# A second Strassen level in the up product of a fused attention and expert kernel

## The chip, the cores and the metric

The kernel runs on one core of a Trainium2 chip. The metric is the device time of one execution in microseconds (us); lower is better. Three runs of the kernel before the change gave 1882.01, 1885.54 and 1887.38 us, with a median of 1885.54 us.

## What is computed

The first half is a linear attention: per batch and head a 64x64 matrix `kv`, the queries times it, and a division by the root mean square. The second half sends the 4608 rows of 512 values through four experts, each an up product, a relu and a down product, and adds the four results with weights per row.

```python
kv = np.einsum('bhsd,bhse->bhde', k, v)          # batch 8, heads 8, s 576, d 64
out = np.einsum('bhsd,bhde->bhse', q, kv)
rms = np.sqrt(np.mean(out * out, axis=-1, keepdims=True) + 1e-06)
x = (out / rms * g_norm)                          # then laid out as (4608, 512)
p = domain_probs / (domain_probs.sum(-1, keepdims=True) + 1e-09)
for e in range(4):
    h = np.maximum(x @ w1[e], 0.0)                # 512 -> 1024
    y += p[:, e:e + 1] * (h @ w2[e])              # 1024 -> 512
```

All data is float32, and TensorE is given float32 operands.

## The kernel before

**Chunks and pairs.** The 4608 rows are cut into 9 chunks of 512 (eight batches' first 512 rows, and one chunk of the 64 rows that each batch has left). The work on one expert and one chunk is called a pair here; there are 4 x 9 = 36, numbered `s = 9*e + c`. A pair has an up product (`up`, 512 to 1024) and a down product (`down`, 1024 to 512).

**One Strassen level in both.** Each product is cut in 2x2x2 blocks, and seven block products take the place of eight (the Winograd form, with few additions). For this the operands are needed in sums: `weights_1` and `weights_2` form four sums of 1024 columns for each of the two weights of an expert, `x_forms` four sums of 512 columns for each chunk's x. The x operands of a chunk, seven tiles of 512 columns, are made once, during the first expert, stored to DRAM (`x_kept`) and loaded again by `x_again` for the other three.

**Up.** `up` runs over the seven products `m` in the order 1, 2, 6, 5, 7, 4, 3 and over two halves `i` of the hidden units. One such product is four matmuls with 256 moving columns (L624). Two PSUM banks of a half take the seven products: some products add on top of what stands in the bank. ScalarE copies a bank to SBUF after the products 1, 6 and 7 (L655), VectorE adds such a copy to the other bank (`total`, L647), and ScalarE applies the relu (L640). Four sums of 512 columns then form the down product's operands, on VectorE or GpSimd.

**Down.** `down` runs seven products for each of two halves of the rows, each four matmuls with 256 columns (L749). VectorE scales every result and adds it to the accumulator (`merge`, L704, and L700 where it is the first).

**Order.** Nothing is scheduled by a compiler here. Every operation is put into a `Plan` with a key (its due place), a cost for each engine that may do it, and its buffers. `Plan.layout` goes through time with these costs, starts on each free engine the first ready operation by key, within a reach, and hands out buffers from fixed sets (`SLOTS`: `big` tiles of 1024 columns, `small` of 512, PSUM banks `ub`, `db`, `ab`). The program is written in that order, and each engine then works through its own list strictly in turn. The key of a down product of pair s is s + 1, so it runs between the up products of pair s + 1. An operation with the costs of `either` goes to VectorE or to GpSimd, whichever is free first; all these sums have the line L276.

Of the kernel before, what the change touches and what calls it, by code (L numbers as in the profile page):

```python
# [24 lines left out]
class Op:  # L25
    def __init__(self, key, cost, fn, reads, writes, kb):
        self.key, self.cost, self.fn, self.kb = key, cost, fn, kb
        self.bufs = list(dict.fromkeys(list(reads) + list(writes)))
        self.new = []
        self.deps = {}  # L30
        self.start = self.end = self.eng = None


class Plan:
# [10 lines left out]

    def __init__(self):
        self.ops = []

    def add(self, key, cost, fn, reads=(), writes=(), parts=(), kb=0):
# [6 lines left out]
        for b in writes:  # L56
            if not b.writers:
                op.new.append(b)
# [4 lines left out]
        for b in parts:  # L63
            if not b.writers:
                op.new.append(b)
            b.writers.append(op)
# [4 lines left out]
    def layout(self, slots):  # L71
# [15 lines left out]
        def ready(op, eng):  # L87
# [4 lines left out]
            for b in op.bufs:  # L92
                if b.kind is not None and b.ap is None and b not in op.new:
                    return None
# [3 lines left out]
            for b in op.new:  # L98
                if b.kind is not None:
                    need[b.kind] = need.get(b.kind, 0) + 1  # L100
            for k, n in need.items():
                if len(free[k]) < n:
                    return None
# [3 lines left out]
        while left:  # L107
            moved = False
            for eng in todo:
# [8 lines left out]
                for op in pending:  # L118
# [11 lines left out]
                    if eng == "SP":  # L130
                        busy[eng] = t + op.cost[eng]
                        bus = max(bus, t + 1.5) + op.kb / 170.0
# [3 lines left out]
                    for b in op.new:  # L136
                        if b.kind is not None:
# [28 lines left out]
def kernel(  # L166
# [63 lines left out]
    SLOTS = {"big": 20, "small": 46, "kv": 6, "kvbd": 8, "ss": 4, "rt": 4, **BANKS}  # L230
    SHAPE = {"big": 2 * NT, "small": NT, "kv": 2 * KR * D, "kvbd": P, "ss": H, "rt": H}
# [10 lines left out]
        (c, m): dram.tile([P, NT], F32, tag=f"x{c}_{m}", name=f"x{c}_{m}")  # L242
# [9 lines left out]
    def pe(columns, passes=2):  # L252
        return {"PE": passes * columns * 2.02 / 2400 + 0.003}
# [63 lines left out]

    def w1_src(e, dh, uh):
# [7 lines left out]
    def weights_1(e, key, step):  # L326
# [19 lines left out]
        w1f[e] = f  # L346
# [69 lines left out]
    def attention(b, key, span, rem):  # L416
# [3 lines left out]
        for hp in range(NPAIR):  # L420
# [29 lines left out]
            plan.add(at(hp), pe(4 * P, 1), turn, reads=[qt], writes=[bank])  # L450
# [22 lines left out]
            plan.add(at(hp), pe(12 * D), key_values, reads=[kt, vt], writes=[bank])  # L473
# [9 lines left out]
            plan.add(at(hp + 0.4), pe(NT), attend, reads=[qT, kvbd[hp]], writes=[raw])  # L483
# [9 lines left out]
            plan.add(at(hp + 1), pe(4 * P, 1), turn_x, reads=[x], writes=[bank])  # L493
# [26 lines left out]
        plan.add(at(NPAIR - 1), pe(4 * P, 1), turn_rem, reads=[qr], writes=[tb])  # L520
# [7 lines left out]
        def attend_rem(eng):  # L528
# [7 lines left out]
            at(NPAIR), pe(NT), attend_rem, reads=[qTr] + [kvbd[hp] for hp in range(NPAIR)],  # L536
# [13 lines left out]
        plan.add(at(NPAIR + 1), pe(4 * P, 1), turn_xrem, reads=[xr], writes=[xb])  # L550
# [15 lines left out]
    def two(ap):  # L566
        return ap.rearrange("p (k t) -> p k t", k=2)

    def x_forms(c, key, step):
        xh = x_halves(c)  # L570
        f = {m: Buf("small", f"xf{c}_{m}") for m in (5, 6, 7, 4)}
        lo, hi = slice(0, HN), slice(HN, NT)
        views = {
            1: (xh[0], lambda: two(xh[0].ap[:])[:, :, lo]),
            12: (xh[0], lambda: two(xh[0].ap[:])[:, :, hi]),
            2: (xh[1], lambda: two(xh[1].ap[:])[:, :, lo]),
            3: (xh[1], lambda: two(xh[1].ap[:])[:, :, hi]),
        }
        for m in (5, 6, 7, 4):
            views[m] = (f[m], lambda m=m: two(f[m].ap[:]))  # L580
        for j, (o, a, b) in enumerate(((5, 12, 1), (6, 3, 5), (7, 3, 12), (4, 2, 6))):
            combine(
                key + j * step, either(NT), views[o][1], views[a][1], views[b][1], ALU.subtract,
                [views[a][0], views[b][0]], [views[o][0]],
            )
        for m in range(1, 8):
            kept[c, m] = Buf(None, f"kept{c}_{m}")
            plan.add(
                key + 0.5, SPC,
                lambda eng, m=m: nc.sync.dma_start(out=two(x_kept[c, m][:]), in_=views[m][1]()),  # L590
# [240 lines left out]
```

## Time and profile before

| what | value |
|---|---|
| runs | 1882.01, 1885.54, 1887.38 us |
| the profiled execution | 1884.76 us, its span 1883.0 us |
| TensorE weight loads (PEld) busy | 1629.1 us of the span, 9472 of them |
| VectorE (DVE) busy | 624.3 us |
| ScalarE (ACT) busy | 390.9 us |
| GpSimd (POOL) busy | 376.4 us |
| moved by DMA | 178.81 MB |

A row of the page's groups reads: line, engine, operation, tile written and tiles read, shape, count, then busy time in total and mean nanoseconds of one, and after the bar the idle time of the engine just before it with what ended that. A float32 matmul is two TensorE instructions in the trace, called passes here, each with its own weight load; so the 2016 matmuls of `up` are 4032 passes. A matmul's end in the trace is modelled, and consecutive ones overlap; the distance from start to start tells how fast they follow each other.

### The profile page before, as it was taken

The page shows a single profiled execution, that of the slowest core. Times are in us where ns is not written, and L with a number is a line of the kernel's source. Part 1 is how long each engine was busy: PE and PEld are TensorE (multiplying, and loading weights), DVE is VectorE, ACT ScalarE, POOL GpSimd, SP SyncE. Part 2 cuts the span into 40 slices and gives each one's busy share as a digit, 9 for nine tenths or more (in the row PEclk, how much of TensorE's full clock was granted, in tenths as well). Part 3 has the DMA queues.
Part 4 walks back from the last instruction along what each step waited for, and adds up shares of the span by engine and source line. Part 5 has one row for each costly group of instructions (what it writes and reads, how often), then busy time and mean ns, then how long its engine had stood idle before and what let it go on. Part 6 is the DMA issues. An engine that isn't in the chain of part 4 may idle for free.

```text
span 1883.0 us, 23222 instructions
## 1 busy us (share of the span) xinstructions
PE 1858.1 (99%) x9472; PEld 1629.1 (87%) x9472; DVE 624.3 (33%) x978; ACT 390.9 (21%) x697; POOL 376.4 (20%) x277
## 2 busy tenths in 40 slices
PE   6999999999999999999999999999999999999999
PEld 5888888888888888888888888888888888888887
DVE  3433333333333333333333223323333333323323
ACT  2433322332111111111111111111111111111110
POOL 2523232224222111111222100001222111111111
PEclk7999999999999999999999999999999999999999
DMA  9544233314232222222322222222332222222111
GB/s 235 154 138 129 78 114 109 105 42 151 73 118 84 84 84 84 84 84 94 109 102 94 77 80 84 80 83 95 118 129 84 84 84 84 84 84 84 45 34 34
DMA packets 142074, 178.81 MB, mean 95 GB/s; under 512 B 49424, under 2 KB 76816, under 8 KB 141968
## 3 DMA queue, kind: packets, MB, share of 16 engines
q1 hardware_dynamic: 141968, 177.33, 29.6%
q8 instruction: 75, 1.23, 0.3%
q14 instruction: 31, 0.25, 0.0%
HBM read 123.02 MB, written 54.26 MB: 94 GB/s over the span
## 4 chain that ended last, share of the span: by engine, by line
PE 97%; SPq 2%; DMA 1%; issue 0%; DVE 0%
PE ub L624 46%; PE db L749 29%; PE ab L749 17%; SPq L282 1%; PE ab L481 1%; PE ab L463 1%; PE ab L491 1%; PE ab L448 1%; PE ab L530 0%; DMA big<-in_moe_w_dram 0%; DMA small<-in_q_dram 0%; SPq L298 0%; PE ab L545 0%; PE ab L515 0%; DVE small L409 0%
## 5 line engine op out<-in xcount | busy, mean ns | idle before, releaser
L624 PE MATMUL ub<-small,big 128*128 128x256 f32 x3600 | 852.4, 380 | 0.0
L624 PEld LDWEIGHTS ub<-small,big 128*128 128x128 f32 x3600 | 681.5, 190 | 93.3 <-issue 0.9
L749 PE MATMUL db<-big,small 128*128 128x256 f32 x2520 | 596.0, 380 | 0.0
L749 PEld LDWEIGHTS db<-big,small 128*128 128x128 f32 x2520 | 475.3, 190 | 64.2 <-issue 0.6
L276 POOL TENSOR_TENSOR small<-small,small 128x512 f32<-128x512 f32 x145 | 210.0, 1456 | 1071.9 <-ACT small L640 1066.3
L749 PE MATMUL ab<-big,small 128*128 128x256 f32 x1512 | 356.2, 379 | 0.0
L749 PEld LDWEIGHTS ab<-big,small 128*128 128x128 f32 x1512 | 287.3, 190 | 39.1
L655 ACT ACTIVATE small<-ub 128x512 f32<-128x512 f32 x216 | 128.8, 597 | 681.4 <-PE ub L624 671.7
L704 DVE SCALAR_TENSOR_TENSOR small<-db,p_all,small 128x256 f32<-128x256 f32 x243 | 117.4, 483 | 453.7 <-PE db L749 453.6
L276 DVE TENSOR_TENSOR small<-ub,small 128x512 f32<-128x512 f32 x216 | 149.4, 692 | 270.3 <-PE ub L624 139.3
L640 ACT ACTIVATE small<-small 128x512 f32<-128x512 f32 x216 | 136.0, 630 | 463.0 <-DVE small L276 463.0
L704 DVE SCALAR_TENSOR_TENSOR small<-ab,p_all,small 128x256 f32<-128x256 f32 x189 | 91.4, 484 | 310.3 <-PE ab L749 310.3
L276 DVE TENSOR_TENSOR small<-small,small 128x512 f32<-128x512 f32 x143 | 160.6, 1123 | 4.6 <-ACT small L640 2.5
L276 POOL TENSOR_TENSOR big<-big,big 128x1024 f32<-128x1024 f32 x26 | 61.1, 2352 | 189.8 <-PE ub L624 105.0
L624 PE MATMUL ub<-big,big 128*128 128x256 f32 x384 | 91.7, 383 | 0.0
L624 PEld LDWEIGHTS ub<-big,big 128*128 128x128 f32 x384 | 71.7, 192 | 9.4 <-issue 0.2
L640 ACT ACTIVATE small<-ub 128x512 f32<-128x512 f32 x72 | 43.0, 597 | 152.1 <-PE ub L624 152.1
L402 POOL TENSOR_TENSOR rt<-ss,mhalf 128x8 f32<-128x8 f32 (+1 forms) x40 | 65.5, 1637 | 3.3
L700 DVE TENSOR_SCALAR small<-db,p_all 128x256 f32<-128x256 f32 x72 | 34.8, 483 | 90.8 <-PE db L749 90.8
L393 DVE TENSOR_REDUCE ss<-small 128x8 f32<-128x512 f32 (+1 forms) x40 | 27.4, 684 | 94.1 <-ACT small L388 94.1
L398 POOL TENSOR_SCALAR ss<-ss 128x8 f32<-128x8 f32 (+1 forms) x40 | 9.4, 236 | 199.3 <-DVE ss L393 198.7
L388 ACT ACTIVATE small<-ab 128x512 f32<-128x512 f32 (+1 forms) x40 | 23.8, 596 | 68.3 <-PE ab L481 54.5
(45 smaller groups left out, 405.7 us busy)
## 6 DMA issues: line engine op xcount, KB each, us to landing
small<-x SPq DMA_DIRECT2D x189, 256.0 KB, 4.3
o<-small SPq DMA_DIRECT2D x108, 256.0 KB, 2.0
small<-o SPq DMA_DIRECT2D x108, 256.0 KB, 3.7
big<-in_moe_w_dram SPq DMA_DIRECT2D x32, 512.0 KB, 5.2
small<-in_q_dram SPq DMA_DIRECT2D x72, 128.0 KB, 3.3
kv<-in_k_dram SPq DMA_DIRECT2D x32, 288.0 KB, 3.4
kv<-in_v_dram SPq DMA_DIRECT2D x32, 288.0 KB, 4.1
x<-small SPq DMA_DIRECT2D x36, 256.0 KB, 2.6
```

The source lines that it names most:

```text
L276: lambda eng: adder(eng).tensor_tensor(out=out_(), in0=a(), in1=b(), op=op),
L282: key, SPC, lambda eng: nc.sync.dma_start(out=dst(), in_=src), reads=reads,
L388: lambda eng: nc.scalar.activation(out=sq.ap[0:n, :], in_=raw.ap[0:n, :], func=ACT.Square),
L393: lambda eng: nc.vector.reduce_sum(out=ss.ap[0:n, :], in_=rows(sq), axis=AX.X),
L402: nc.gpsimd.tensor_tensor(out=rt.ap[0:n, :], in0=ss.ap[0:n, :], in1=mhalf[0:n, :], op=ALU.pow)
L448: nc.tensor.transpose(bank.ap[:, rs], qt.ap[:, rs], ident[:])
L624: nc.tensor.matmul(ps.ap[:, u * HN:(u + 1) * HN], lhsT=two(w1f[e][m].ap[:])[:, kt, cols], rhs=views[m][1]()[:, kt, :], start=(m in (1, 2, ...
L640: lambda eng: nc.scalar.activation(out=b.ap[:], in_=src.ap[:], func=ACT.Relu),
L655: lambda eng, to=banks[i, -m], ps=ps: nc.scalar.activation(out=to.ap[:], in_=ps.ap[:], func=ACT.Copy),
L700: nc.vector.tensor_scalar_mul(out=acc[i].ap[:, cols], in0=ps.ap[:, 0:HN], scalar1=prob)
L704: nc.vector.scalar_tensor_tensor(out=acc[i].ap[:, cols], in0=ps.ap[:, 0:HN], scalar=prob, in1=acc[i].ap[:, cols], op0=ALU.mult, op1=ALU.add,)
L749: nc.tensor.matmul(ps.ap[:, 0:HN], lhsT=src[:, kt % 2, t * P:(t + 1) * P], rhs=w2f[e][m].ap[:, kt * HN:(kt + 1) * HN], start=(m in (1, 2, ...
```

## The change

The up product gets a second Strassen level inside the first. Each of the seven block products of a pair is itself cut in 2x2x2 blocks, now over all 512 hidden units of the block, and computed with seven products of two matmuls with 128 moving columns. A pair has 49 of them.

- **Operands.** `weights_1` forms, for each of the seven outer operands, four more sums of 256 columns: two in place of raw quarters, three results in a new tile `w1y` of 768 columns. `x_forms` forms four more sums of 128 columns for each of the seven x operands (tile `xt`), 28 a chunk. `x_kept` has seven blocks of 128 columns instead of four; `x_again` loads two tiles for each operand, of 384 and 512 columns.
- **Evacuation.** For each outer product ScalarE makes four copies of 256 columns out of PSUM (L710) and VectorE three additions of 256 columns (L718) into one `big` tile.
- **Outer sums.** What the first level did inside PSUM is now done in SBUF: 11 sums of 1024 columns a pair on VectorE or GpSimd (`add` in `up`), which include the forms for the down product, and four relus of 1024 columns (L680).
- **Buffers and the layout.** `big` 28 instead of 20, `small` 22 instead of 46, new sets `w1y` (7) and `snap` (5). The layout may not take the last four `big` or `small` tiles for an operation that lies ahead of TensorE's place, and a buffer gets its slot at its first started writer. The bus of loads is reckoned at 215 instead of 170 kB per us. `down` only reads `h` through another view, and a merge now decides at its place in the order whether it is the first.

The core of the diff:

```diff
@@ Plan
+    SPARE = {"big": 4, "small": 4}
...
             for k, n in need.items():
-                if len(free[k]) < n:
+                if len(free[k]) < n + (self.SPARE.get(k, 0) if op.key > front + 0.1 else 0):
                     return None
...
-                        bus = max(bus, t + 1.5) + op.kb / 170.0
+                        bus = max(bus, t + 1.5) + op.kb / 215.0
@@ buffers
-    SLOTS = {"big": 20, "small": 46, "kv": 6, "kvbd": 8, "ss": 4, "rt": 4, **BANKS}
+    SLOTS = {
+        "big": 28, "w1y": 7, "kv": 4, "small": 22, "snap": 5, "kvbd": 8, "ss": 4, "rt": 4, **BANKS
+    }
...
-        (c, m): dram.tile([P, NT], F32, tag=f"x{c}_{m}", name=f"x{c}_{m}")
+        (c, m): dram.tile([P, 7 * P], F32, tag=f"x{c}_{m}", name=f"x{c}_{m}")
@@ weights_1
+        for j, m in enumerate(OUTER):
...
+            k2 = key + (8 + j) * step
+            for o, a, b, op in (
+                (5, 7, 4, ALU.add), (7, 1, 7, ALU.subtract), (6, 5, 1, ALU.subtract),
+                (3, 2, 6, ALU.subtract),
+            ):
+                combine(
+                    k2, either(HN), parts[o][1], parts[a][1], parts[b][1], op,
+                    [parts[a][0], parts[b][0]], [parts[o][0]],
+                )
@@ x_forms
+        for j, m in enumerate(OUTER):
...
+            for o, a, b in ((5, 12, 1), (6, 3, 5), (7, 3, 12), (4, 2, 6)):
+                combine(
+                    key + (4 + j) * step, either(P), parts[o][1], parts[a][1], parts[b][1],
+                    ALU.subtract, [parts[a][0], parts[b][0]], [parts[o][0]],
+                )
@@ up
-        for j, m in enumerate(ORDER):
-            for i in range(2):
...
-                    for u in range(2):
-                        cols = slice((2 * i + u) * P, (2 * i + u + 1) * P)
-                        for kt in range(2):
-                            nc.tensor.matmul(
-                                ps.ap[:, u * HN:(u + 1) * HN],
-                                lhsT=two(w1f[e][m].ap[:])[:, kt, cols], rhs=views[m][1]()[:, kt, :],
+        for i, m in enumerate(OUTER):
+            whole = made[m] = Buf("big", f"m{n}")
+            bank = {1: Buf("ub", f"u1_{n}"), 2: Buf("ub", f"u2_{n}")}
+            for j, mm in enumerate(ORDER):
+                key = s + (i + j / 7) / 7
+                if mm == 5:
+                    bank[2] = Buf("ub", f"u3_{n}")
+                ps = bank[1 if mm in (1, 6, 7, 4) else 2]
...
+                    for u in range(2):
+                        nc.tensor.matmul(
+                            ps.ap[:, u * P:(u + 1) * P],
+                            lhsT=w1f[e][m][mm][1]()[:, u * P:(u + 1) * P], rhs=views[m][mm][1](),
...
+                if mm in (1, 6, 7):
+                    snap[mm] = Buf("snap", f"s{mm}_{n}")
+                    copy(snap[mm], lambda b=snap[mm]: b.ap[:])
+                if mm == 2:
+                    total(0, 0, ps, snap[1])
+                elif mm == 7:
+                    total(1, 1, bank[2], snap[7])
+                elif mm == 4:
+                    copy(whole, lambda whole=whole: block(whole, 1, 0))
+                elif mm == 3:
+                    total(0, 1, ps, snap[6])
+            key = s + (i + 1) / 7
...
+            if m == 2:
+                add(key, unit(1), made[1], made[2])
+                relu(key, h[1])
+            elif m == 6:
+                add(key, made[1], made[1], made[6])
+            elif m == 5:
+                add(key, made[6], made[1], made[5])
+            elif m == 3:
+                add(key, unit(21), made[6], made[3])
+                relu(key, h[21])
+                add(key, unit(7), h[1], h[21], ALU.subtract)
+            elif m == 7:
+                add(key, made[1], made[1], made[7])
+                add(key, unit(4), made[1], made[5])
+                relu(key, h[4])
+                add(key, unit(5), h[21], h[4])
+                add(key, unit(6), h[5], h[1], ALU.subtract)
+            elif m == 4:
+                add(key, unit(2), made[1], made[4])
+                relu(key, h[2])
+                add(key, unit(3), h[2], h[6], ALU.subtract)
```

### Where the instructions stand

In the rows below a name with a number is one buffer: `ub`, `db` and `ab` are PSUM banks, `small` and the first name after it on an up row are x and weight operands, `x4` or `x2` at the end counts matmuls.

TensorE before, in a pair of the second expert; an up row (L624) alternates with a product of `down` (L749, here in two rows of two):

```order
L624 MATMUL ub3_163<-small36_128,big19_91 128x256 x4
L749 MATMUL ab0_166<-big8_80,small29_121 128x256 x2
L749 MATMUL ab0_166<-big8_80,small22_114 128x256 x2
L624 MATMUL ub0_160<-small27_119,big18_90 128x256 x4
L749 MATMUL ab1_167<-big12_84,small44_136 128x256 x2
L749 MATMUL ab1_167<-big12_84,small2_94 128x256 x2
L624 MATMUL ub1_161<-small27_119,big18_90 128x256 x4
```

TensorE after, in a pair of the second expert (L697 is `up`, L831 `down`):

```order
L831 MATMUL ab1_161<-big18_90,big2_74 128x256 x4
L697 MATMUL ub1_155<-small16_127,big1_73 128x128 x2
L697 MATMUL ub0_154<-small5_116,big13_85 128x128 x2
L697 MATMUL ub2_156<-small5_116,big13_85 128x128 x2
L831 MATMUL ab0_160<-big11_83,big19_91 128x256 x4
L697 MATMUL ub1_155<-small16_127,big1_73 128x128 x2
L697 MATMUL ub3_157<-small4_115,w1y5_105 128x128 x2
L697 MATMUL ub0_154<-small8_119,w1y2_102 128x128 x2
L697 MATMUL ub2_156<-small8_119,w1y2_102 128x128 x2
L831 MATMUL ab1_161<-big5_77,big20_92 128x256 x4
L697 MATMUL ub0_154<-small8_119,big13_85 128x128 x2
```

Two outer products are under way at a time, with two banks each. Between two uses of a bank by consecutive products (`ub0` in rows 3, 8 and 11, `ub2` in rows 4 and 9) there now stand two or three up rows and one down row.

VectorE after, in the first pair of the third expert: evacuations (L718), merges (L788) and outer sums (L276) in one list. `big8` in the sixth row is `h21`, whose relu on ScalarE lies between that row and the eighth.

```order
L788 SCALAR_TENSOR_TENSOR small21_132<-ab1_161,p_all_69,small21_132 128x256
L718 TENSOR_TENSOR big0_72<-ub1_155,snap2_135 128x256
L718 TENSOR_TENSOR big20_92<-ub0_154,snap0_133 128x256
L788 SCALAR_TENSOR_TENSOR small5_116<-ab0_160,p_all_69,small5_116 128x256
L718 TENSOR_TENSOR big0_72<-ub1_155,snap3_136 128x256
L276 TENSOR_TENSOR big8_80<-big9_81,big0_72 128x1024
L788 SCALAR_TENSOR_TENSOR small5_116<-ab1_161,p_all_69,small5_116 128x256
L276 TENSOR_TENSOR big21_93<-big19_91,big8_80 128x1024
L718 TENSOR_TENSOR big20_92<-ub0_154,snap4_137 128x256
L718 TENSOR_TENSOR big0_72<-ub1_155,snap2_135 128x256
L788 SCALAR_TENSOR_TENSOR small5_116<-ab1_161,p_all_69,small5_116 128x256
```

Before, no sum of 1024 columns stood among these; now each is a longer row in front of the evacuations behind it.

VectorE before at the start, between the second and the last scaling of x (L409) of the first chunk:

```order
L409 TENSOR_TENSOR small18_110<-ab0_166,rt1_157 128x512
L393 TENSOR_REDUCE ss2_154<-small20_112 128x8
L409 TENSOR_TENSOR small22_114<-ab1_167,rt2_158 128x512
L276 TENSOR_TENSOR big11_83<-big2_74,big3_75 128x1024
L276 TENSOR_TENSOR big12_84<-big11_83,big0_72 128x1024
L276 TENSOR_TENSOR big13_85<-big1_73,big12_84 128x1024
L393 TENSOR_REDUCE ss3_155<-small24_116 128x8
L409 TENSOR_TENSOR small26_118<-ab0_166,rt3_159 128x512
```

The same place after the change, its first twelve rows of thirty (L432 is the scaling, `ss2` the third head pair's reduction):

```order
L432 TENSOR_TENSOR small17_128<-ab0_160,rt1_151 128x512
L276 TENSOR_TENSOR w1y1_101<-big1_73 128x256
L276 TENSOR_TENSOR big9_81<-big0_72,big2_74 128x1024
L276 TENSOR_TENSOR w1y2_102<-big9_81 128x256
L276 TENSOR_TENSOR big9_81<-big9_81 128x256
L276 TENSOR_TENSOR w1y2_102<-w1y2_102,big9_81 128x256
L276 TENSOR_TENSOR w1y3_103<-big3_75 128x256
L276 TENSOR_TENSOR w1y2_102<-big9_81,w1y2_102 128x256
L276 TENSOR_TENSOR w1y4_104<-big10_82 128x256
L276 TENSOR_TENSOR big3_75<-big3_75 128x256
L276 TENSOR_TENSOR w1y3_103<-w1y3_103,big3_75 128x256
L276 TENSOR_TENSOR w1y3_103<-big3_75,w1y3_103 128x256
```

Between the two scalings there are now 2 sums of 1024 columns and 23 of 256 on VectorE, where there were 3 of 1024 columns.

218 lines of the change are left out of this document (117 added, 101 removed).

## The prediction, made before the changed kernel was run

> **What bounds the kernel now.** I read the page's busy times and slices first, then the chain, then stretches of the span, then TensorE's waits.
>
> ```profile
> span 1883.0 us, 23222 instructions
> PE 1858.1 (99%) x9472; PEld 1629.1 (87%) x9472; DVE 624.3 (33%) x978; ACT 390.9 (21%) x697; POOL 376.4 (20%) x277
> PEclk7999999999999999999999999999999999999999
> PE 97%; SPq 2%; DMA 1%; issue 0%; DVE 0%
> ...
> 20.00:30.00 10.00, 6.01 (x56) 5.35 (x57) 3.14 (x3) 2.85 (x7) 4.14 (x3) 0.67 1.16 262
> 30.00:40.00 10.00, 5.32 (x36) 4.75 (x35) 5.09 (x6) 2.20 (x6) 3.43 (x4) 0.50 0.81 202
> 60.00:100.00 40.00, 38.71 (x316) 33.62 (x315) 18.61 (x27) 16.88 (x36) 21.87 (x21) 1.00 0.59 150
> 520.00:1000.00 480.00, 480.00 (x2226) 422.55 (x2225) 152.92 (x239) 84.95 (x140) 82.23 (x50) 1.00 0.28 95
> ...
> PE ab L491 <- DVE small L409: 10.4, 4, 4.1
> ```
>
> In the stretch rows the columns are PE, weight loads, DVE, ACT, POOL, clock, DMA. TensorE is the bound: 99% busy, 97% of the chain, granted its full clock after the start. Busy is no proof of full speed, but the stretch from 520 to 1000 us is: 2226 passes in 480 us, **215.6 ns a pass**, all of 256 columns, with no gap. TensorE idles only in the first 60 us and a little to 100; its largest wait is 10.4 us there, for x. So time comes off only by fewer or shorter passes, and is lost wherever another engine makes TensorE wait. VectorE has 152.92 of 480 us in work, 32%.
>
> **TensorE's own work.** The up product's rows:
>
> ```profile
> L624 PE MATMUL ub<-small,big 128*128 128x256 f32 x3600 | 852.4, 380 | 0.0
> L624 PE MATMUL ub<-big,big 128*128 128x256 f32 x384 | 91.7, 383 | 0.0
> L624 PE MATMUL ub<-x_rem,big 128*128 128x256 f32 x48 | 11.3, 379 | 0.0
> ```
>
> That is 4032 passes, 112 for each of 36 pairs; at 215.6 ns they take 869.3 us. After, a pair has 49 products x 2 matmuls x 2 passes = 196 passes of 128 columns, 7056 in all. They are seven eighths of the columns, so at half the pass time the gain would be 869.3 / 8 = 108.7 us. But each pass needs its own 128x128 weights, with half the time to load them behind. The trace has just this shape: the attention product L481, 128x128 weights and 128 columns.
>
> ```profile
> 227.56 1.05 PE L481 MATMUL ab<-kvbd,small 128*128 128x128 f32 x8
> 228.46 1.89 PE L749 MATMUL db<-big,small 128*128 128x256 f32 x8
> ...
> 266.47 1.05 PE L481 MATMUL ab<-kvbd,small 128*128 128x128 f32 x8
> 267.36 1.89 PE L749 MATMUL db<-big,small 128*128 128x256 f32 x8
> ...
> L481 PEld LDWEIGHTS ab<-kvbd,small x256: 186/192/337, 10.4 to 423.7; 128*128 128x128 f32 x128
> 215.90 1.08 PEld L481 LDWEIGHTS ab<-kvbd,small 128*128 128x128 f32 x8
> ```
>
> Eight passes take 0.90 and 0.89 us from the first start to the start of the next group: 111 to 112.5 ns each. I take **112 ns**: 7056 x 0.112 = 790.3 us, a gain of **79.0 us** (75.5 at 112.5 ns; 86 at 111). The 4032 passes of `down` and the attention stay as they are. A load lasts 192 ns, yet eight of them fit into 1.08 us, so consecutive loads overlap.
>
> The Trainium skill speaks against the change here: Perfetto Trace Analysis, Identifying the Most-Contended Engine, judges TensorE's headroom by the summed LDWEIGHTS time over the window. By that measure, 12496 loads of 192 ns would be 2399 us, more than the span; the last row disagrees, eight loads of 192 ns (1.54 us) in 1.08 us.
>
> **What is added to the other engines.** Prices:
>
> ```profile
> L276 DVE TENSOR_TENSOR small<-big 128x512 f32<-128x512 f32 x6 | 4.2, 692 | 5.4 <-ACT big L497 5.4
> 42.09 1.22 DVE L276 TENSOR_TENSOR big<-big,big 128x1024 f32<-128x1024 f32 x1
> L276 DVE TENSOR_TENSOR small<-ub,small 128x512 f32<-128x512 f32 x216 | 149.4, 692 | 270.3 <-PE ub L624 139.3 <-ACT small L655 128.0 <-DMA small<-in_q_dram 1.0
> L704 DVE SCALAR_TENSOR_TENSOR small<-db,p_all,small 128x256 f32<-128x256 f32 x243 | 117.4, 483 | 453.7 <-PE db L749 453.6
> L523 ACT ACTIVATE small<-ab 128x256 f32<-128x256 f32 x8 | 3.1, 382 | 3.3 <-PE ab L515 3.1
> L655 ACT ACTIVATE small<-ub 128x512 f32<-128x512 f32 x216 | 128.8, 597 | 681.4 <-PE ub L624 671.7
> L640 ACT ACTIVATE small<-small 128x512 f32<-128x512 f32 x216 | 136.0, 630 | 463.0 <-DVE small L276 463.0
> L276 POOL TENSOR_TENSOR big<-big,big 128x1024 f32<-128x1024 f32 x26 | 61.1, 2352 | 189.8 <-PE ub L624 105.0
> ```
>
> From 692 ns at 512 columns and 1.22 us at 1024, a VectorE sum of 256 is an estimated 0.43 us. From 382 and 597 ns, a relu of 1024 is 0.63 + 2 x 0.215 = 1.06 us. The order gives 343 of the 428 sums of 1024 columns (396 of `up`, 32 of weights) to VectorE, 85 to GpSimd. A pair then costs VectorE 21 x 0.43 + 14 x 0.483 + 9.5 x 1.22 = 27.4 us and ScalarE 28 x 0.382 + 4 x 1.06 = 14.9 us, against 196 x 0.112 + 112 x 0.2156 = 46.1 us of TensorE: 59% and 32%. Throughput holds; what is new is that TensorE waits on banks sooner.
>
> ```profile
> 1001.19 1.89 PE L624 MATMUL ub<-small,big 128*128 128x256 f32 x8
> 1003.12 0.60 ACT L655 ACTIVATE small<-ub 128x512 f32<-128x512 f32 x1 [2.80 <-PE ub L624]
> ...
> 47.67 0.69 DVE L276 TENSOR_TENSOR small<-ub,small 128x512 f32<-128x512 f32 x1 [0.62 <-PE ub L624]
> 48.40 0.63 ACT L640 ACTIVATE small<-small 128x512 f32<-128x512 f32 x1 [2.06 <-DVE small L276]
> ```
>
> A copy starts 0.04 us after the modelled end of the last pass (1003.08), which for L481's shape lies 0.15 us after its slot (227.56 + 1.05 = 228.61 against 228.46); engine to engine takes another 0.04. So product 7, copy, addition, back to TensorE is 0.15 + 0.04 + 0.38 + 0.04 + 0.43 + 0.05 = 1.09 us. The order has mostly three up rows and one down row in between, 3 x 0.448 + 1.725 = 3.07 us. Slack: 2.0 us. A sum of 1.22 us standing ahead of the addition fits in; so I cost the **later pairs at 0**, hidden by that slack. Gone it costs 1 us of the run for every 1/36 us a pair loses.
>
> What can exceed it is shown here:
>
> ```profile
> 48.28 4.16 DVE L276 TENSOR_TENSOR big<-big,big 128x1024 f32<-128x1024 f32 x1
> 49.01 2.34 POOL L276 TENSOR_TENSOR big<-big,big 128x1024 f32<-128x1024 f32 x1
> L276 DVE TENSOR_TENSOR small<-small,small 128x512 f32<-128x512 f32 x143 | 160.6, 1123 | 4.6 <-ACT small L640 2.5
> ```
>
> VectorE's 1.22 us sum takes 4.16 us around a GpSimd sum, and the 143 sums average 1123 ns instead of 692. Sums with both operands in SBUF exclude each other on the two engines; additions from PSUM don't (the 216 of the price rows average 692). The Trainium skill says so (SBUF — State Buffer, Who interferes with whom): a VectorE instruction with two SBUF inputs and a GpSimd one that reads SBUF take a shared port in turn, whole instructions long. The trace agrees, 4.16 against 1.22 us. A full hold makes 1.22 + 2.35 = 3.57 us, 1.6 over the slack. In later pairs GpSimd has about one such sum a pair, mostly with none of VectorE's close behind it. Three places are denser:
>
> - **First expert**, 9 chunks: 28 sums of 128 and 4 of 512 more or less at once per chunk, split over both engines, beside the attention. Bounds: 0, if the slack takes all, to 40 us (a hold of 2.35 us twice a chunk, all on TensorE). I take 10, nearer to 0, because before, 143 x 0.43 = 61 us of holds cost TensorE nothing from 100 us on.
> - **Three expert changes**: 28 sums of 256 and 8 of 1024 each. 0 to 12 us; I take 4.
> - **Start**:
>
> ```profile
> 19.22 0.69 DVE L409 TENSOR_TENSOR small<-ab,rt 128x512 f32<-128x512 f32 x1 [2.04 <-POOL rt L402]
> 36.96 0.69 DVE L409 TENSOR_TENSOR small<-ab,rt 128x512 f32<-128x512 f32 x1 [2.04 <-POOL rt L402]
> 37.71 1.12 PE L491 MATMUL ab<-ident,small 128*128 128x128 f32 x4 [4.14 <-DVE small L409]
> 39.47 2.51 PE L624 MATMUL ub<-big,big 128*128 128x256 f32 x8
> ```
>
> The first up product starts at 39.47 us, behind the last scaling of chunk 0's x. VectorE's list between the second scaling (ended 19.22 + 0.69 = 19.9 us) and the last (36.96) now holds 23 x 0.43 + 2 x 1.22 + 4 x 0.69 = 15.1 us, behind which the attention's reductions and scalings queue, with GpSimd sums of some 10 us that exclude them. 19.9 + 15.1 = 35 us if all overlaps with the old waits, 45 if nothing does; and 28 sums of 128 columns follow. Bounds -2 to +20; I take **+8**.
>
> **DMA and the rest.** x loads double in number, 14 a pair, 192 and 256 KB.
>
> ```profile
> small<-x SPq DMA_DIRECT2D x189, 256.0 KB, 4.3
> ```
>
> The order leaves at least 38 us of passes between a load and its first product, against 4.3 us to landing: 0. Traffic grows by 37 MB of loads and 12 of stores, to about 125 GB/s, under the 262 of the row from 20 to 30 us.
>
> **Sum.** The profiled execution took 1884.8 us (span 1883.0 and 1.8 around it), 0.04% under the median. 1884.8 - 79.0 + 8 + 10 + 4 = 1827.8, **1828 us**.
>
> **Rivals.**
>
> - *TensorE hardly waits* (slack takes everything): 1884.8 - 79 - 2 = 1804, or 1797 at 111 ns. For it: no wait after 100 us before. Against it: bank uses stand 3.07 us apart or less, and the start's queue. 15%.
> - *Holds reach TensorE*: each of the 85 GpSimd sums holds VectorE, 0.5 us of it past the slack: +43, over 1806 + 14 (start, expert changes, first chunks without them): 1863. The port row speaks for it, the thin overlap in later pairs against. 13%.
> - *Slower: VectorE's list stalls on the relu.* Where h21, h4 or h2 is formed, the next sum at the head of the list waits 1.06 + 0.1 us for ScalarE, and every addition behind it stands still. Three a pair, 0.7 us each uncovered, and 1.4 holds of 0.7 us: 3 us. If all of it reached TensorE, 36 x 3 = 108: 1806 + 14 + 108 = 1928. It decides from (79 - 22) / 36 = 1.6 us a pair, and the slack of 2.0 us is against it. 8%.
> - *Weight loads don't overlap in long rows*: 7056 x 0.192 = 1355 us, +486: about 2390. From 123 ns a pass (869.3 / 7056) the change loses. L481's rows, at 112, are against it. 2%.
>
> That the passes aren't saved is no rival: the order counts them.
>
> **How the numbers follow.** The forecast (1810 to 1848) has 62%. The range takes in the first rival down to 1797 and the holds up to 1868, leaving the slower cases and the worst holds out: 1797 to 1868. Within 0.3% (1879 to 1891), about what a measurement of this kernel can tell from no change, only the worst holds fall: 3%. Slower: 10% (the relu stalls 8, the weight loads 2). Faster: 87%.
>
> **What would show it.** Right: up passes 112 ns apart in the later pairs, 7056 of them; TensorE without waits between 520 us and the end; the first up product between 40 and 48 us; VectorE near 60% there. Wrong: waits of L697 for L718 or L710 in every pair; VectorE sums near 3.5 us in later pairs; passes over 115 ns apart without a named wait; waits of L697 on `x` loads.

## The result and the profile after

The changed kernel takes 1820.63 us (median of four runs, 1820.08 to 1821.06) against 1883.99 us before (median of four, 1882.01 to 1887.38): a ratio of 0.9662, with a 95% interval of 0.9645 to 0.9678. The forecast was 1828 us, in a range of 1797 to 1868. The profiled execution took 1820.08 us, its span 1818.3 us.

The page of the changed kernel, its span, busy times, clock, chain and the groups that answer to those before:

```profile
span 1818.3 us, 32290 instructions
PE 1784.6 (98%) x12496; PEld 1660.7 (91%) x12496; DVE 1126.2 (62%) x1841; ACT 608.4 (33%) x1345; POOL 475.1 (26%) x426
PEclk7999999999999999999999999999999999999999
PE 94%; DVE 2%; SPq 2%; DMA 1%; issue 1%; POOL 0%; ACT 0%; DVEq 0%; ACTq 0%
...
L697 PE MATMUL ub<-small,big 128*128 128x128 f32 x3816 | 513.5, 276 | 0.4 <-DVE big L718 0.4
L276 DVE TENSOR_TENSOR big<-big,big 128x1024 f32<-128x1024 f32 x343 | 474.8, 1384 | 55.1 <-ACT big L680 33.2
L276 POOL TENSOR_TENSOR big<-big,big 128x1024 f32<-128x1024 f32 x85 | 209.0, 2462 | 1116.7 <-DVE big L276 976.1
L710 ACT ACTIVATE snap<-ub 128x256 f32<-128x256 f32 x756 | 285.5, 383 | 556.7 <-PE ub L697 500.8
L718 DVE TENSOR_TENSOR big<-ub,snap 128x256 f32<-128x256 f32 x756 | 307.0, 421 | 216.7 <-PE ub L697 163.1
L680 ACT ACTIVATE big<-big 128x1024 f32<-128x1024 f32 x144 | 152.0, 1055 | 107.8 <-DVE big L276 104.8
```

TensorE is still the bound, and it has 12496 passes instead of 9472. VectorE has gone from 33 to 62% of the span, as the sums had it (59% in a pair), and still stands outside the chain but for 2%. The additions out of PSUM take 421 ns each, while the 343 sums with both operands in SBUF average 1384 ns where 1.22 us was the undisturbed price. These are holds by GpSimd, as the experiment with all sums on VectorE shows.

Stretches of the changed kernel (columns PE, weight loads, DVE, ACT, POOL, clock, DMA share, GB/s), and its waits of TensorE, longest in total first:

```profile
0.00:60.00 60.00, 37.26 (x287) 32.47 (x288) 41.29 (x74) 17.72 (x39) 33.48 (x40) 0.79 0.95 238
60.00:100.00 40.00, 37.27 (x345) 34.26 (x344) 29.74 (x47) 20.22 (x46) 22.20 (x16) 0.97 0.49 117
520.00:1000.00 480.00, 479.09 (x3197) 448.40 (x3195) 297.50 (x475) 150.23 (x331) 107.43 (x70) 1.00 0.40 128
1400.00:1790.00 390.00, 390.00 (x2607) 365.45 (x2607) 234.20 (x382) 123.09 (x271) 26.75 (x12) 1.00 0.36 109
...
PE ab L514 <- DVE small L432: 9.4, 4, 4.3
PE ab L471 <- DMA small<-in_q_dram: 5.8, 1, 5.8
PE ub L697 <- DVE big L718: 5.2, 3, 2.7
```

From 1400 to 1790 us, 2607 passes fill 390 us without a gap. A pair has 196 + 112 = 308 passes, so 46.08 us; the 112 passes of `down` at 215.6 ns leave 21.93 us, or **111.9 ns for an up pass**.

To see where time went, I price every TensorE pass of both traces at its undisturbed distance (215.6 ns for 256 columns, 112 for 128, 33 to 70 for the attention's small ones) and subtract the sum from each stretch. What is left, in us, is time in which TensorE had no work or was slower than these prices:

| stretch, us | before | after | difference |
|---|---|---|---|
| 0 to 60 | 31.0 | 37.5 | +6.5 |
| 60 to 100 | 2.8 | 6.3 | +3.5 |
| 100 to 440 (the rest of the first expert) | 10.0 | 11.4 | +1.4 |
| 440 to 960 (with the first two expert changes) | 0.5 | 2.8 | +2.3 |
| 960 to 1420 (with the third) | 0.6 | 1.6 | +1.0 |
| 1420 to 1780 | 0.4 | -0.3 | -0.7 |
| 1780 to the end | 4.9 | 5.1 | +0.2 |
| all | 50.2 | 64.4 | +14.2 |

With the price of the passes, 79.0 us less, this makes 1883.0 - 79.0 + 14.2 = 1818.2 us, the span. That sum comes out by construction; the table says only where the 14.2 us lie. (Some 10 us of 100 to 440 are there in both, while TensorE is busy for 340.0 and 339.5 of the 340 us; they are the attention's small passes, priced too low. The -0.7 us is within what the rounded prices can tell from nothing.)

The first two rows are not idle time alone. After the change the granted clock is 0.50 from 22 to 45 us and again from 59.2 to 62.6 us, before it was 0.50 from 17 to 23 and from 28 to 40 us, and passes are slower there: the eight up passes from 41.76 us (in the timeline below) take 1.84 us to the next row of TensorE, 230 ns each. Counted at one more full price for each pass begun at half clock, this is an estimated 6.2 us before and 8.3 us after, 2.1 of the 10.0 us that the start lost.

### The profile page after: what moved, and what is told of

Its sections match the earlier page's. It is cut to its first block, busy times and chain, and to the rows that moved or that the text cites. A ratio compares the mean times of both kernels' runs of the same rounds, so it can differ in the third digit from the quotient of the medians.

```text
span 1818.3 us, 32290 instructions
## 1 busy us (share of the span) xinstructions
PE 1784.6 (98%) x12496; PEld 1660.7 (91%) x12496; DVE 1126.2 (62%) x1841; ACT 608.4 (33%) x1345; POOL 475.1 (26%) x426
## 4 chain that ended last, share of the span: by engine, by line
PE 94%; DVE 2%; SPq 2%; DMA 1%; issue 1%; POOL 0%; ACT 0%; DVEq 0%; ACTq 0%
PE ub L697 42%; PE db L831 29%; PE ab L831 18%; SPq L282 1%; PE ab L504 1%; PE ab L486 1%; DVE big L276 1%; PE ab L514 1%; PE ab L471 1%; DVE small L276 0%; DMA big<-in_moe_w_dram 0%; DMA small<-in_q_dram 0%; PE ab L553 0%; DVE big L718 0%; POOL big L276 0%
## 5 line engine op out<-in xcount | busy, mean ns | idle before, releaser
L831 PE MATMUL db<-big,big 128*128 128x256 f32 x2520 | 596.3, 380 | 1.7 <-DVE big L276 1.3
L697 PEld LDWEIGHTS ub<-small,big 128*128 128x128 f32 x3816 | 498.4, 192 | 23.4 <-issue 1.4
L697 PE MATMUL ub<-small,big 128*128 128x128 f32 x3816 | 513.5, 276 | 0.4 <-DVE big L718 0.4
L276 DVE TENSOR_TENSOR big<-big,big 128x1024 f32<-128x1024 f32 x343 | 474.8, 1384 | 55.1 <-ACT big L680 33.2
L831 PEld LDWEIGHTS db<-big,big 128*128 128x128 f32 x2520 | 455.2, 190 | 51.7 <-DVE big L276 1.5
L276 POOL TENSOR_TENSOR big<-big,big 128x1024 f32<-128x1024 f32 x85 | 209.0, 2462 | 1116.7 <-DVE big L276 976.1
L710 ACT ACTIVATE snap<-ub 128x256 f32<-128x256 f32 x756 | 285.5, 383 | 556.7 <-PE ub L697 500.8
L718 DVE TENSOR_TENSOR big<-ub,snap 128x256 f32<-128x256 f32 x756 | 307.0, 421 | 216.7 <-PE ub L697 163.1
L697 PE MATMUL ub<-small,w1y 128*128 128x128 f32 x2916 | 384.9, 276 | 2.2 <-DVE big L718 2.1
L697 PEld LDWEIGHTS ub<-small,w1y 128*128 128x128 f32 x2916 | 360.5, 192 | 7.9 <-DVE big L718 2.9
L831 PE MATMUL ab<-big,big 128*128 128x256 f32 x1512 | 357.4, 380 | 1.7 <-DVE small L788 1.7
L831 PEld LDWEIGHTS ab<-big,big 128*128 128x128 f32 x1512 | 273.2, 190 | 32.0 <-DVE small L788 2.1
L710 ACT ACTIVATE big<-ub 128x256 f32<-128x256 f32 x252 | 96.7, 384 | 414.6 <-PE ub L697 410.1
L788 DVE SCALAR_TENSOR_TENSOR small<-db,p_all,small 128x256 f32<-128x256 f32 x243 | 116.9, 481 | 139.8 <-PE db L831 139.2
L788 DVE SCALAR_TENSOR_TENSOR small<-ab,p_all,small 128x256 f32<-128x256 f32 x189 | 91.1, 482 | 177.3 <-PE ab L831 177.3
L680 ACT ACTIVATE big<-big 128x1024 f32<-128x1024 f32 x144 | 152.0, 1055 | 107.8 <-DVE big L276 104.8
L432 DVE TENSOR_TENSOR small<-ab,rt 128x512 f32<-128x512 f32 (+1 forms) x40 | 27.4, 686 | 17.3 <-POOL rt L425 17.1
```

What stands on the lines that cost most here:

```text
L276: lambda eng: adder(eng).tensor_tensor(out=out_(), in0=a(), in1=b(), op=op),
L432: lambda eng: nc.vector.tensor_tensor(out=rows(x), in0=rows(raw), in1=rt.ap[0:n, :].unsqueeze(2).to_broadcast([n, H, D]), op=ALU.mult,),
L680: lambda eng: nc.scalar.activation(out=b.ap[:], in_=b.ap[:], func=ACT.Relu),
L697: nc.tensor.matmul(ps.ap[:, u * P:(u + 1) * P], lhsT=w1f[e][m][mm][1]()[:, u * P:(u + 1) * P], rhs=views[m][mm][1](), start=(mm in (1, 2, ...
L710: lambda eng: nc.scalar.activation(out=where(), in_=ps.ap[:, 0:HN], func=ACT.Copy),
L718: lambda eng: nc.vector.tensor_tensor(out=block(whole, a, t), in0=src.ap[:, 0:HN], in1=add_.ap[:], op=ALU.add),
```

## The experiments

Beside these runs the kernel before took 1885.4 to 1885.7 us (medians). Stretches "without work" are reckoned as in the table above.

### What makes a pass 112 ns long

Half of the columns are taken from four of the seven inner products; the output lacks what they would have given.

```diff
-                            ps.ap[:, u * P:(u + 1) * P],
-                            lhsT=w1f[e][m][mm][1]()[:, u * P:(u + 1) * P], rhs=views[m][mm][1](),
+                            ps.ap[:, u * P:u * P + (P if mm in (1, 2, 5) else 64)],
+                            lhsT=w1f[e][m][mm][1]()[:, u * P:(u + 1) * P],
+                            rhs=views[m][mm][1]()[:, 0:(P if mm in (1, 2, 5) else 64)],
```

> In the up product the four inner products that add to a bank (6, 7, 4, 3) stream 64 of their 128 columns; the other 64 columns are left out, while weights, copies and waits stay. This narrows 4032 of the 7056 up passes. Theory A, the weight load sets the 112 ns: the narrowed passes stay 107 to 112 ns apart and the run takes 1800 to 1822 us. Theory B, the streaming of the columns sets it: they stand some 57 ns apart, 4032 x 0.055 = 222 us less, about 1600 us or as far down as VectorE allows.

One run took 1817.95 us. The stretch of this kernel that answers to the third row above, same columns:

```profile
520.00:1000.00 480.00, 478.99 (x3201) 448.53 (x3200) 298.34 (x475) 150.24 (x331) 105.98 (x69) 1.00 0.40 127
```

3201 passes in 480 us, where it was 3197: with 4032 passes cut to half their columns, this one run is shorter by 2.7 us, not by 222. Theory A holds. A pass with new 128x128 float32 weights costs 112 ns with 64 columns as with 128. Nor is it a fixed cost of every pass: in the changed kernel 24 passes of the attention with weights of 96x64 and 64 columns take 0.85 us to the next row, 35 ns each.

```profile
62.80 0.92 PE L486 MATMUL ab<-kv,kv 96*64 96x64 f32 x24
63.65 1.16 PE L697 MATMUL ub<-small,big 128*128 128x128 f32 x8
```

### Is the gain in the passes or in the layout

The kernel before gets the planner of the changed one (its classes Op and Plan), of which these are the main lines (also, a buffer gets its slot at its first started writer):

```diff
+    SPARE = {"big": 4, "small": 4}
...
-                if len(free[k]) < n:
+                if len(free[k]) < n + (self.SPARE.get(k, 0) if op.key > front + 0.1 else 0):
...
-                        bus = max(bus, t + 1.5) + op.kb / 170.0
+                        bus = max(bus, t + 1.5) + op.kb / 215.0
```

> The kernel before with the new Plan alone (the spare tiles, the bus at 215, slots at the first started writer), its products as they were. Theory A, the gain is in the passes of the up product: within 3 us of the kernel before. Theory B, part of it comes from the layout: 5 us or more faster.

1883.35 us, a ratio of 0.9992 (0.9983 to 1.0002) to the kernel before. The layout's new rules give nothing by themselves, so the gain is in the passes.

### Do VectorE and GpSimd still cost TensorE time in the later pairs

First all outer sums go to VectorE:

```diff
-                key, either(2 * NT), lambda: to.ap[:], lambda: a.ap[:], lambda: b.ap[:], op,
+                key, dve(2 * NT), lambda: to.ap[:], lambda: a.ap[:], lambda: b.ap[:], op,
```

> All 396 outer sums on VectorE, none on GpSimd. Theory A, in the later pairs the slack takes the holds and VectorE's load: the pairs stay at 46.05 us, the run within 2 us of 1820.6; VectorE near 66% busy. Theory B, holds by GpSimd sums still cost TensorE something: 3 to 6 us less, most of it at the expert changes, where 3 to 4 us are lost now. Theory C, VectorE's list is near its limit: 5 us or more slower.

1821.3 us, ratio 0.9656 (0.9641 to 0.9670): theory A for the run. From 1420 to 1780 us GpSimd has nothing to do now, and VectorE's 86 sums of 1024 columns average 1221 ns there; in the changed kernel 77 of them average 1290 ns beside eight sums of GpSimd. So the holds are GpSimd's, and TensorE works through all 360 us with them and without. A part of theory B is there too: from 500 us to the end there are 6.4 us without work, 9.0 in the changed kernel, so about 2.6 us were lost to holds, mostly at the expert changes. The run gains nothing, since the first expert loses 4 more instead (15.4 against 11.4); why is not shown.

Then they go to the two engines by turns:

```diff
-                key, either(2 * NT), lambda: to.ap[:], lambda: a.ap[:], lambda: b.ap[:], op,
+                key, (gp if len(plan.ops) % 2 else dve)(2 * NT),
+                lambda: to.ap[:], lambda: a.ap[:], lambda: b.ap[:], op,
```

> The outer sums fixed by turns to VectorE and GpSimd, so that GpSimd has 215 sums of 1024 columns instead of 85. Theory A, the slack in front of TensorE takes the holds: VectorE's sums of 1024 columns get longer still (mean over 1.7 us instead of 1.38), but the later pairs stay near 46.05 us and the run within 10 us of 1820.6. Theory B, holds reach TensorE by half a microsecond or more each: 130 more of them, 65 us or more slower.

1831.79 us, ratio 0.9719 (0.9705 to 0.9734), 11 us over the changed kernel. The groups of sums on this kernel's page:

```profile
L276 POOL TENSOR_TENSOR big<-big,big 128x1024 f32<-128x1024 f32 x215 | 520.8, 2426 | 889.2 <-DVE big L719 647.5
L276 DVE TENSOR_TENSOR big<-big,big 128x1024 f32<-128x1024 f32 x213 | 289.8, 1367 | 13.5 <-POOL big L276 3.8
```

GpSimd has 520.8 us of these sums instead of 209.0. Theory B's 65 us are excluded; theory A's 10 us were slightly too few, and its longer VectorE sums didn't come, since VectorE has fewer of them to be held (1367 ns, against over 1.7 us expected). Of the loss 5.5 us each are in 500 to 860 and 960 to 1320 us (instead of 1.2 and 0) and 4.5 more than in the changed kernel are in 100 to 440. From 1420 to 1780 us nothing is lost, with GpSimd busy for 107.3 us instead of 18.9. The 5.5 us are single waits and what follows them. Two rows of its timeline of TensorE, with the idle time before each in brackets:

```profile
505.96 3.16 PE L832 MATMUL db<-big,big 128*128 128x256 f32 x8 [1.96 <-DVE big L276]
557.01 1.99 PE L832 MATMUL db<-big,big 128*128 128x256 f32 x8 [1.26 <-POOL big L276]
```

The first waits for a VectorE sum that took 3.25 us beside GpSimd, the second for a GpSimd sum; between 960 and 1320 us there is one wait, 3.87 us for an addition out of PSUM before 974.80 us. After the first and the last of these the granted clock is 0.58 and 0.57 over the next four microseconds (506 to 510 and 974 to 978 us), and 1.00 again after them.

### Where the slack comes from

```diff
-    CROSS, SAME = 0.3, 0.06
+    CROSS, SAME = 0.05, 0.03
```

> The layout reckons 0.05 us instead of 0.3 us for a handover between engines (0.03 within one), so that operations are put closer behind each other; the work is the same. Theory A, these 0.3 us are part of the slack that takes the holds: TensorE now waits for additions and copies in most pairs, the run 5 to 40 us slower. Theory B, the distance between two uses of a bank comes from the turn of up and down products alone: within 2 us of 1820.6.

1842.72 us, ratio 0.9779 (0.9764 to 0.9793): 22 us slower with the same amount of work. Theory A's size is right, and B falls. But A's mechanism is not what the trace shows: TensorE doesn't wait in most pairs, it has a few long waits. Three rows of its waits (us in total, times, longest):

```profile
PE ab L504 <- ACT kvbd L494: 8.3, 5, 4.0
PE ub L697 <- DVE big L718: 5.2, 5, 1.6
PE ab L831 <- DVE small L788: 5.1, 2, 2.6
```

Without work are 2.4 us more before 100, 6.5 more from 100 to 440, 5.1 more from 500 to 860, 4.7 more from 960 to 1320, and nothing more from 1420 to 1780 us; the rest is around the expert changes. The new layout also has another order and gives GpSimd 106 sums instead of 85, so part of the loss may be theirs; that was not told apart. Shown is that the layout planned with 0.3 us is 22 us faster than the one planned with 0.05, and not that these 0.3 us are what takes up the holds in the later pairs.

### What makes the start longer

The changed kernel's start, from its timeline: GpSimd, VectorE and TensorE in turn.

```profile
20.36 4.84 POOL L276 TENSOR_TENSOR big<-big,big 128x1024 f32<-128x1024 f32 x2
21.04 1.95 DVE L276 TENSOR_TENSOR w1y<-big 128x256 f32<-128x256 f32 x1
22.91 3.37 DVE L276 TENSOR_TENSOR big<-big,big 128x1024 f32<-128x1024 f32 x1
31.06 0.68 DVE L416 TENSOR_REDUCE ss<-small 128x8 f32<-128x512 f32 x1
53.33 3.38 DVE L305 TENSOR_SCALAR tot<-tot 128x36 f32<-128x36 f32 x1
...
54.34 2.33 POOL L276 TENSOR_TENSOR big<-big,big 128x1024 f32<-128x1024 f32 x1
...
41.76 1.91 PE L697 MATMUL ub<-big,big 128*128 128x128 f32 x8
57.85 0.71 PE L697 MATMUL ub<-big,w1y 128*128 128x128 f32 x4 [2.74 <-DVE big L718]
```

Two sums of VectorE are held by GpSimd's pair of sums for 1.5 and 2.1 us, the third reduction of x comes at 31.06 us (24.82 before), the first up product at 41.76 (39.47 before), and at 57.85 us TensorE waits 2.74 us for an addition out of PSUM that stands behind the held operation of L305 (3.38 us for 36 columns). Four experiments ask which of these is the cause: the holds, the place in the list, that one operation, or the amount of work.

The holds: the first expert's weight sums on VectorE alone.

```diff
-                k_, either(1024), lambda: f[o].ap[:], lambda: f[a].ap[:], lambda: f[b].ap[:], op,
+                k_, (either if e else dve)(1024), lambda: f[o].ap[:], lambda: f[a].ap[:], lambda: f[b].ap[:], op,
...
-                    k2, either(HN), parts[o][1], parts[a][1], parts[b][1], op,
+                    k2, (either if e else dve)(HN), parts[o][1], parts[a][1], parts[b][1], op,
```

> The 32 sums of the first expert's up weights on VectorE alone, none on GpSimd. Theory A, the holds between the two engines made the start late: VectorE's sum of 1024 columns at 22.9 us no longer takes 3.37 us, the first up product starts 2 to 4 us before 41.8 us, and the run is 2 to 4 us shorter. Theory B, the amount of VectorE work made it late: two sums of 1024 and some of 256 columns more in its list, 3 to 5 us, start the first up product 2 to 4 us later and lengthen the run by as much.

1819.96 us, ratio 0.9651 (0.9637 to 0.9666). The first up product starts at 40.18 us, 1.6 earlier, yet 43.7 us without work lie before 100 us, as in the changed kernel (43.8). Neither theory: the holds went (VectorE's four sums of 1024 columns from 21 to 28 us take 1.22 us each, and the operation of L305 0.18 us), but TensorE still waits 2.80 us for an addition out of PSUM, at 52.96 us. What took their place is not shown: VectorE has the work that GpSimd no longer does, and the granted clock is 0.50 from 53 to 62 us, longer than after the change.

The place in the list: the inner sums due with the product that uses them.

```diff
-            k2 = key + (8 + j) * step
+            k2 = key + (8 + j) * step if e else -0.2 + j / 7
```

> The 28 inner sums of the first expert's up weights become due with the outer product that uses them, instead of all ahead of the first. Theory A, the attention's reductions and scalings of chunk 0 stand behind them in VectorE's list: the third reduction comes at 25 to 27 us instead of 31.06, the first up product at 38 to 40 us instead of 41.8, and the run is 2 to 5 us shorter. Theory B, the work is only moved: the first up product comes earlier, but the time is lost again before 100 us, and the run stays within 1 us of 1820.6.

1825.13 us, ratio 0.9679 (0.9663 to 0.9695). The third reduction comes at 27.06 us and the first up product at 36.46, earlier than theory A said, and the run is 4.5 us longer. Theory B was right that the time is lost again, but its 1 us was too mild: 46.4 us without work before 100 us. The row of the longest wait of its TensorE timeline, and of the VectorE operation that leads to it:

```profile
63.22 1.20 PE L697 MATMUL ub<-small,w1y 128*128 128x128 f32 x4 [4.82 <-DVE big L718]
...
55.86 4.07 DVE L305 TENSOR_SCALAR tot<-tot 128x36 f32<-128x36 f32 x1
```

That one operation: the addition of 1e-9 to 36 columns, done on GpSimd. (In the plan it becomes an operation of its own, between VectorE's before and after it.)

```diff
-            nc.vector.tensor_scalar_add(out=tot[:], in0=tot[:], scalar1=1e-9)
+            nc.gpsimd.tensor_scalar(
+                out=tot[:], in0=tot[:], scalar1=1.0, scalar2=1e-9, op0=ALU.mult, op1=ALU.add,
+            )
```

> The addition of 1e-9 to the 36 sums of the probabilities, which took 3.38 us on VectorE at 53.3 us around a GpSimd sum, is done on GpSimd. Theory A, this hold made TensorE's wait of 2.74 us at 57.85 us: that wait goes and the run is 2 to 3 us shorter, about 1818. Theory B, VectorE's list is full there in any case and the time is lost elsewhere before 100 us: within 1 us of 1820.6.

1821.87 us (1820.28 to 1822.04), ratio 0.9665 (0.9651 to 0.9680). The waits of its TensorE (its lines stand nine further down):

```profile
PE ab L523 <- DVE small L441: 12.7, 5, 4.2
PE ab L495 <- DMA kv<-in_v_dram: 4.1, 2, 2.2
PE ub L706 <- DVE big L727: 3.2, 4, 1.1
```

The wait for additions went from 5.2 to 3.2 us and the one for scalings from 9.4 to 12.7: the time is lost elsewhere, as theory B said, though the run lies 1.3 us over 1820.6 and not within 1.

The amount of work: the 28 inner sums of the first expert's weights are left out, and raw quarters multiplied in their place.

```diff
+            if not e:
+                for n, (uq, kt) in ((5, (0, 0)), (6, (0, 1)), (3, (1, 0))):
+                    parts[n] = (x, lambda x=x, uq=uq, kt=kt: two(x.ap[:])[:, kt, uq * HN:(uq + 1) * HN])
+                w1f[e][m] = parts
+                continue
```

> The 28 inner sums of the first expert's up weights are left out; the products take raw quarters in their place. Theory A, the start is as long as VectorE and GpSimd need for the sums in it: 28 x 0.34 us of work less, of the 43.8 us that the first 100 us hold beside TensorE's work 5 to 9 go, the run 1811 to 1816 us. Theory B, the start hangs on the attention's chain of engine after engine, and the sums fit between: within 2 us of 1820.6.

1815.33 us, ratio 0.9627 (0.9614 to 0.9640): 5.5 us less than the changed kernel on the same chip, and 38.4 us without work before 100 us instead of 43.8. Theory A. Of the four changes only this one, which takes work away, makes the start clearly shorter; giving the work to the other engine, making it due later or moving the one operation doesn't. It is not one for one: 28 sums at 0.34 us are 9.5 us of VectorE and GpSimd, and 5.5 us came off.

### A version with the work taken out of the start

If it is the work, it must not stand in the start. Pair 0 does its up product with one level, out of PSUM by ScalarE alone, so that VectorE has none of its 21 additions; the inner sums of the first expert's weights and of chunk 0's x become due during it, and the stores of chunk 0's x later too.

```diff
+            for a in range(2 if s == 0 else 0):
+                key = s + (i + a / 2) / 7
+                ps = Buf("ub", f"u{a}_{n}")
...
+                plan.add(key, pe(4, HN), plain, reads=[raw1[e][m], src], writes=[ps])
...
+                plan.add(
+                    key - 0.4, {"ACT": 0.83}, out_of, reads=[ps], parts=[whole],
+                )
...
-            for j, mm in enumerate(ORDER):
+            for j, mm in enumerate(ORDER if s else ()):
...
             up(s, e, x_views.pop(s))
+            if s == 0:
+                inner_1(0, -0.2, 0.1)
```

> Pair 0 alone does its up product as before, with one level (56 matmuls of 256 columns, two copies of ScalarE for each half product, no additions on VectorE); the first expert's inner weight sums and chunk 0's inner x sums become due during that pair and not ahead of it. TensorE has 112 x 0.2156 - 196 x 0.112 = 2.2 us more. Theory A, the start is bound by the sums: 6 to 9 us of the 43.8 go, the run 3 to 7 us shorter than 1820.6. Theory B, the work is only moved, as when it was made due later: 1 to 4 us longer.

1813.78 us (1811.25 to 1815.38), ratio 0.9621 (0.9608 to 0.9634). Beside it the changed kernel was run again:

> The changed kernel once more, on the chip of the other runs of this call: 1819 to 1823 us, ratio 0.966 by every theory.

1820.8 us (1818.18 to 1821.08), ratio 0.9653 (0.9640 to 0.9666). So the version with one level in pair 0 beats both kernels, by 7.0 us of medians over the changed one. Its first two stretches, same columns as above:

```profile
0.00:60.00 60.00, 39.81 (x309) 32.94 (x310) 36.69 (x64) 20.80 (x48) 30.14 (x32) 0.91 0.95 238
60.00:100.00 40.00, 39.34 (x326) 34.70 (x324) 36.09 (x57) 20.96 (x50) 29.52 (x31) 1.00 0.66 168
```

VectorE's 41.29 us in the first 60 are now 36.69, and it is busier from 60 to 100 us, 36.09 us instead of 29.74, where TensorE hardly waits for it. The first up product starts at 33.82 us, and 33.7 us without work lie before 100 us, against 43.8 in the changed kernel and 33.8 before the change. In this trace all of the 10 us are back, for 2.2 us of longer passes; it is the quickest of the five runs, 1811.25 us. The passes begun at half clock, reckoned as above, are an estimated 4.7 us of the 33.7, where they were 8.3 of the 43.8, so a part of the gain comes through the clock; how much was not told apart.

## Why the prediction was right, step by step

- **What bounds it.** Right: TensorE without a gap in the later pairs of both kernels, so that the price of its passes decides.
- **The pass at 112 ns.** Right: 111.9 ns measured. The reason given, that the load of the weights is the floor and not the columns, was only argued from L481's rows; with 64 columns, and with the attention's 35 ns, it is shown. The gain is 79 us, not the 108.7 of seven eighths of the columns.
- **Weight loads.** The 12496 loads of the trace add up to 2348 us (2399 at 192 ns each) within a span of 1818.3, so their sum is no bound here. By the measure of the Trainium skill (Perfetto Trace Analysis, Identifying the Most-Contended Engine), the summed load time over the window, the change could not have paid. The trace disagrees: that sum is 129% of the span, since loads overlap one another.
- **Later pairs at 0.** Right: -0.7 us from 1420 to 1780 us, and neither with all sums on VectorE nor with five times as many on GpSimd do the pairs there get longer. Nearer the expert changes a little is lost: from 520 to 1000 us TensorE is busy for 479.09 of 480 us. Something takes up the holds; that it is the slack between two uses of a bank, as the prediction reckoned it, was argued and not tested by itself.
- **First expert, +10.** This is the step that was mis-sized: 1.4 us measured from 100 to 440 us. The holds are there. Added up over VectorE's sums in that stretch, the time beyond the shortest sum of the same size is 28.6 us, but nearly none of it reaches TensorE. I had bounded it by TensorE's share of the holds and taken a quarter of that; the row it should have followed was the other one, 61 us of holds before that cost nothing.
- **Expert changes, +4.** Right in sum: +2.3 and +1.0 us, with 500 to 860 us counted in.
- **Start, +8.** Right in size, 10.0 us, and partly by luck; first up product at 41.8 us, within the 40 to 48 named. The reason was half right. I put it on the attention's operations queueing behind the weight sums; but with these sums due later the first up product came earlier and the run still got longer, and only taking work out of the start took time off. The amount of work of VectorE and GpSimd is what the runs show. Some 2 of the 10 us are passes at half clock, for which the prediction had no term.
- **DMA at 0.** Right: no wait of TensorE for an x load stands among its waits, at a mean of 126 GB/s.

The 7 us between 1828 and 1820.6 are the first expert's term (8.6 us too high), with 2.0 us from the start against it and 0.7 from the expert changes with it. Of the rivals, the shortest one (1804) fell by the start. The holds and the relu stalls are there (VectorE stands idle 33.2 us in all before its sums of 1024 columns, for the relu), but hardly reach TensorE.

## What to carry to other kernels

Price a smaller tile by a row of the same shape, and ask whether its weight load or its columns set the pace: here halving the columns of four of the seven inner products saved next to nothing. Work that goes from the bound engine to others is free only where these have room, and in this kernel the first tens of microseconds, in which every operand is formed, had none; a cheaper variant of the first step alone gave that back. When a list is planned ahead, try a cautious handover time in the plan: without it the layout here was 22 us slower.

## What was not expected

- A float32 pass with new 128x128 weights takes 112 ns with 64 moving columns as with 128.
- An addition of one constant to 36 columns on VectorE took 3.38 and 4.07 us beside GpSimd sums, with a single operand in SBUF; before it took 1.04 us, and 0.18 us with the first expert's weight sums on VectorE alone.
- VectorE operations behind each other overlap: from 26.78 to 29.25 us, sums of 256 columns with 0.42 us of busy time start every 0.34 us. The prediction priced them at 0.43.

```profile
26.78 0.42 DVE L276 TENSOR_TENSOR big<-big 128x256 f32<-128x256 f32 x1
27.12 0.42 DVE L276 TENSOR_TENSOR w1y<-w1y,big 128x256 f32<-128x256 f32 x1
27.46 0.42 DVE L276 TENSOR_TENSOR w1y<-big 128x256 f32<-128x256 f32 x1
```

- A wait of TensorE in the middle of the run can cost more than itself: in the run with the sums by turns, two waits of 1.96 and 3.87 us were each followed by some 3.4 us at half of the granted clock, which with the waits makes most of the 5.5 us lost in each of the two stretches. Not every wait was followed so: after one of 2.10 us at 84.41 us in the changed kernel the clock stays at 1.00.
